# Pooled attention and a feed-forward block on one core: scores of token tile 12 issued before the PSUM pools change, and some 380 other steps placed elsewhere

## The chip, the core and the metric

The kernel runs on one core of one Trainium2 chip. The metric is the device time of one execution in microseconds (us). Five engines work beside each other, each through its own queue in order: TensorE (PE, with its weight loads as PEld), VectorE (DVE), ScalarE (ACT), GpSimd (POOL), and SyncE (SP), which here issues transfers. L790 and the like are lines of the kernel's code.

## What is computed

The inputs are q, k and v with 8 batches, 8 heads, 576 positions and 64 channels, a gain `moe_g_ln` of 512, and two weight matrices, 512 x 2048 and 2048 x 512.

```
k_p, v_p = means of k and of v over groups of 8 positions        # 72 positions
scores   = (q @ k_p.T) / sqrt(64);  scores -= scores.max(-1)
attn     = exp(scores) / (exp(scores).sum(-1) + 1e-9)
x        = (attn @ v_p), heads side by side                      # 4608 tokens x 512
xn       = (x - mean) / sqrt(var + 1e-6) * g_ln
out      = x + relu(xn @ w_ch1) @ w_ch2
```

## The kernel before

**Tiles.** The 4608 tokens are 36 tiles of 128; four tiles make a chunk of 512, so there are nine chunks, c = 0 to 8. The two large products keep float32 accuracy with float16 operands: each operand is split into a high and a low half, and three matmuls stand for one.

**Two lists of steps.** The order of all work is written out by hand, in two strings of tokens, START (the opening, 760 tokens) and STEADY (3404 tokens). A token such as `P.2.0.0.2` names a step and its arguments; each step is a Python generator, and each time that its token stands in the list, `run` (L1410) lets it issue its next piece. So the list gives the order in which every engine's queue receives its instructions, and no engine overtakes its own queue.

**The opening** loads and splits the weights (`R` loads, `C` converts, `M1`, `M2` and `S.m.b` scale and split with ACT L483 and DVE L490), pools the first k and v (`HK`, `HV`), and takes chunks 0 and 1 through with plain products: `F.c.f` is the first product (L1116) and its relu halves (ACT L1125, DVE L1127), `G.c.tt.half` the second (L1319) and its DVE sum into x (L1330).

**The loop over chunks 2 to 8** replaces each large product by seven of half size: `P.c.h.f.m` is one of the seven of the first product (`product`, six matmuls of 256 columns at L1160, then one copy on ACT at L1179 or a sum on DVE at L1174 or L1177 out of PSUM), `EL`, `ER`, `ES`, `EP` build the factors of the second from it (DVE and POOL at L1198, ACT L1196), and `O.c.h.n.u` is one of the seven of the second (`out_seven`, twelve matmuls at L1277, then a DVE sum into x at L1294). Several of the seven share one PSUM tile, so the next product that uses a tile can only start when the copy or sum of the one before has read it.

**Attention.** `A.t` is `stage_a` (L1338) of token tile t: its first piece loads q of tile t + 2, the second issues the 16 score matmuls (L790), the third the row maximum (DVE L800) and the subtraction (DVE L805), and later pieces the exponential, the halves and a transposing transfer. `B.t` is `stage_b`: the matmuls with v, the normalisation (DVE L939 to L961) and what layer norm needs. `TS`, `TW`, `T`, `U`, `WH`, `Z`, `XT` prepare scales and sums of operands.

**PSUM.** The opening uses four pools: `ps_s` for scores and `ps_x`, two banks each, `ps_f` with three and `ps_m` with one. Between the two lists `first.close()` gives them back, and two new pools take the space: `ps_a`, one buffer of two banks (scores and values of the loop), and `ps_g`, six (all products). What the first tile of a new pool writes over must have been read by then.

```
    run(START)
    first.close()
    for name, bufs in (("ps_a", 1), ("ps_g", 6)):
        psum[name] = ctx.enter_context(tc.tile_pool(name=name, bufs=bufs, space=PSUM))
    psum["ps_s"] = psum["ps_x"] = psum["ps_a"]
    psum["ps_f"] = psum["ps_m"] = psum["ps_g"]
    run(STEADY)
```

Of the kernel before, what the change touches and what calls it, by code (L numbers as in the profile page):

```python
# [63 lines left out]
START = """  # L64
LN.2 Q.0 LK.0 LN.2 LK.1 R.1.0 Q.1 A.0 R.1.1 R.1.2 K0 V0 K0 A.0 R.1.3 A.0 A.0 K0 R.1.3 R.1.2 HV.1.0 LK.0 LK.1 LG V0 R.2.0
E.0.0 LG V0 C.1.0 C.1.0 C.1.0 C.1.0 R.2.0 E.0.0 E.0.0 V0 V0 E.0.1 A.1 A.1 V0 A.1 E.1.0 C.1.1 V0 Q.1 C.1.1 E.0.1 C.1.1
C.1.1 E.0.0 V0 V0 C.1.2 C.1.3 E.0.1 C.1.2 E.1.0 E.0.1 E.1.1 HV.1.0 E.1.1 HV.1.0 E.1.1 C.1.3 E.1.1 E.1.0 HV.1.0 E.1.0
R.2.1 HV.1.0 HK.1.0 R.2.1 A.2 A.2 M1.0 A.2 A.2 B.0 A.1 M1.0 M1.0 M1.0 S.1.0 E.2.0 B.0 S.1.0 C.2.0 S.1.1 C.1.2 R.1.1 B.0
E.2.1 Q.0 HV.1.0 S.1.0 A.3 E.2.1 E.2.0 A.3 A.3 C.1.3 S.1.1 HK.1.0 E.2.1 A.3 E.2.0 E.2.1 B.0 B.0 B.0 B.0 S.1.2 E.2.0
R.1.0 B.1 HK.1.0 R.2.2 E.3.0 B.1 R.2.2 E.3.1 E.3.0 E.3.1 E.3.0 E.3.1 B.1 B.1 B.1 B.1 B.1 C.1.3 E.3.1 E.3.0 HV.1.0 C.2.0  # L70
HK.1.0 C.1.2 S.1.2 B.2 B.2 HV.1.1 C.2.2 S.1.3 HV.1.1 C.2.1 B.2 HV.1.0 B.2 B.2 C.2.0 B.2 B.2 S.1.3 HK.1.0 C.2.0 S.1.3 B.3
HK.1.1 HK.1.1 S.1.2 HK.1.1 C.2.1 HK.1.1 HK.1.1 C.2.1 C.2.1 B.3 F.0.0.0 F.0.1.0 F.0.0.0 F.0.1.0 F.0.0.0 R.2.3 D.0 R.2.3
F.0.1.0 A.4 F.0.0.0 F.0.2.0 A.4 F.0.1.0 F.0.3.0 A.4 HV.1.0 HV.1.1 C.2.2 HV.1.1 B.3 C.2.3 F.0.2.0 F.0.3.0 F.0.2.0 A.4
F.0.2.0 A.4 F.0.3.0 F.0.3.0 C.2.3 D.0 F.0.4.0 R.1.4 HV.1.1 A.5 A.5 A.5 C.2.2 C.2.2 HV.1.1 HV.1.1 C.2.3 F.0.4.0 B.3 B.3
B.3 B.3 R.1.4 F.0.5.0 A.5 F.0.6.0 R.1.5 M2.0 M2.0 F.0.5.0 F.0.4.0 F.0.6.0 F.0.4.0 A.5 M2.0 M2.0 R.1.6 S.1.1 A.6 S.2.0
A.6 R.1.7 C.1.4 R.1.7 F.0.5.0 A.4 R.1.5 A.4 HV.1.1 F.0.5.0 F.0.6.0 A.6 S.2.0 F.0.7.0 F.0.0.1 HV.1.1 F.0.0.1 F.0.1.1
HV.1.1 HV.1.1 F.0.1.1 F.0.7.0 HV.1.1 F.0.7.0 HV.1.1 HV.1.1 D.1 D.1 S.2.1 F.0.1.1 C.1.4 F.0.0.1 S.2.1 C.1.7 F.0.2.1 S.2.0
A.7 A.7 R.1.6 C.1.5 F.0.3.1 F.0.3.1 F.0.3.1 C.2.3 F.0.2.1 S.2.2 S.2.2 S.2.2 F.0.2.1 F.0.3.1 HV.1.1 F.0.4.1 F.0.2.1
F.0.5.1 C.1.6 M1.1 F.0.4.1 F.0.5.1 F.0.4.1 F.0.5.1 F.0.5.1 C.1.4 A.6 F.0.4.1 F.0.6.1 B.4 A.5 S.2.3 M1.1 B.4 M1.1 F.0.7.0
A.6 C.1.5 S.2.3 F.0.7.1 F.0.7.1 F.0.7.1 F.0.7.1 G.0.0.0 B.4 F.0.0.1 F.0.1.1 F.0.6.1 S.2.3 C.1.4 A.7 F.0.6.1 C.1.5 A.6  # L80
A.6 S.1.4 G.0.0.0 R.2.4 R.2.4 R.2.5 R.2.5 A.7 C.1.7 B.5 B.4 G.0.1.0 F.0.6.1 A.7 A.7 A.7 B.4 G.0.2.0 C.1.6 C.1.7 C.1.6
S.1.4 R.2.6 R.2.7 S.1.5 B.5 B.5 S.1.5 G.0.1.0 R.2.6 R.2.7 G.0.2.0 G.0.2.0 HK.2.0 G.0.3.0 C.2.4 S.1.6 C.2.5 S.1.6 B.6 B.4
C.2.4 G.0.1.0 B.4 S.1.7 G.0.3.0 S.1.7 F.0.8 HV.2.0 G.0.3.0 B.5 C.2.4 B.5 B.5 F.0.8 B.6 F.0.8 F.0.9 C.2.5 B.5 C.2.6
F.0.10 A.5 C.2.7 C.2.6 F.0.8 F.0.9 F.0.9 F.0.6.0 F.0.11 C.2.5 C.2.7 C.2.5 C.2.6 C.2.7 C.2.7 HK.2.0 F.0.10 C.2.6 F.0.11
B.6 C.2.4 C.1.5 M2.1 S.1.4 F.0.9 HK.2.0 F.0.12 M1.1 HK.2.1 F.0.10 A.8 HK.2.1 HK.2.0 HV.2.0 F.0.10 S.1.7 M2.1 M2.1 S.2.4
S.1.5 F.0.11 HV.2.0 F.0.12 S.2.4 F.0.12 A.8 S.2.5 F.0.12 F.0.13 S.2.4 F.0.11 S.2.5 S.2.5 HK.2.0 HV.2.0 HV.2.0 F.0.13 B.6
F.0.14 HV.2.0 C.1.7 HK.2.1 B.7 HV.2.0 G.0.0.0 S.2.6 F.0.14 HK.2.1 F.0.15 B.6 HK.2.1 F.0.13 F.0.13 S.2.6 S.2.7 S.2.7
F.0.14 F.0.14 F.0.15 S.2.7 HV.2.0 F.0.15 C.1.6 B.7 A.8 B.7 F.0.15 HV.2.0 B.7 A.8 HK.3.0 G.0.0.1 HV.2.1 HK.3.0 HV.2.1 B.7
A.8 HV.2.1 HV.2.1 HV.2.1 B.6 A.8 A.9 G.0.1.1 G.0.2.1 S.1.6 HV.2.1 B.6 B.7 HV.2.1 HV.3.0 G.0.0.1 G.0.1.1 A.9 G.0.2.1 B.7
A.8 A.9 A.9 G.0.3.1 A.9 T.1.0 HV.2.1 A.10 A.10 A.11 A.9 G.0.3.1 T.1.0 G.0.3.1 G.0.3.1 HV.2.1 F.1.0 A.9 B.8 T.1.0 T.1.0  # L90
F.1.0 HK.3.0 A.10 G.0.1.1 G.0.1.1 F.1.1 T.1.0 A.11 B.8 T.1.0 F.1.0 HV.2.1 S.2.6 T.1.0 S.2.1 T.1.0 F.1.2 F.1.0 T.1.0 A.10
T.1.0 HV.2.1 F.1.1 T.1.0 T.1.0 HV.2.1 F.1.1 F.1.2 F.1.2 F.1.3 HV.2.1 F.1.4 F.1.2 F.1.5 HV.2.1 HV.3.0 HV.3.0 T.1.1 HV.2.1
HV.2.1 G.0.2.1 F.1.1 F.1.4 F.1.4 G.0.2.1 HV.3.0 F.1.4 F.1.3 HV.3.0 A.10 A.11 A.10 HV.3.0 F.1.3 T.1.1 A.11 HV.3.0 F.1.3
F.1.6 B.9 F.1.6 T.1.1 F.1.5 HV.3.0 HV.3.0 A.10 T.1.1 A.11 HV.3.1 F.1.5 T.1.1 G.0.0.1 F.1.7 T.1.1 A.11 G.0.0.1 F.1.6
F.1.5 HV.3.1 T.1.1 A.11 HV.3.1 T.1.1 F.1.7 F.1.7 G.1.0.0 G.1.0.0 G.1.0.0 B.9 HV.3.1 G.1.1.0 HV.3.1 F.1.6 T.1.1 HV.3.1
G.1.2.0 HV.3.1 T.1.1 T.1.1 M2.1 HK.3.1 T.1.1 T.0.0 T.0.0 T.0.0 T.0.0 HV.3.1 T.0.0 T.0.0 V.10 G.1.3.0 T.0.0 T.0.0 HK.3.0
HK.3.0 T.0.0 T.0.0 F.1.7 T.0.0 G.1.2.0 HV.3.1 T.0.0 F.1.8 T.0.1 G.1.1.0 F.1.9 T.0.1 F.1.8 T.0.1 G.1.3.0 G.1.3.0 T.0.1
V.10 B.8 B.8 T.0.1 T.0.1 T.0.1 T.0.1 F.1.10 HV.3.1 F.1.8 HV.3.1 F.1.8 HV.3.1 T.0.1 F.1.9 U.0.1 U.0.0 F.1.11 F.1.10
F.1.11 F.1.9 T.0.1 F.1.9 B.8 F.1.10 B.11 B.8 F.1.10 U.0.1 G.1.1.0 F.1.12 B.11 U.0.1 T.0.1 F.1.13 F.1.12 T.0.1 F.1.13
F.1.11 F.1.11 F.1.14 F.1.12 F.1.14 F.1.13 F.1.13 B.9 F.1.15 F.1.15 B.9 U.1.1 B.9 U.1.0 F.1.14 F.1.14 F.1.15 F.1.15 B.9  # L100
B.9 V.10 V.10 HV.3.1 V.10 U.1.0 G.1.0.1 V.10 G.1.1.1 HV.3.1 F.1.12 U.1.0 HK.3.1 HK.3.1 V.10 V.10 G.1.2.1 G.1.0.1 X X
B.11 B.11 B.11 B.11 G.1.1.1 G.1.2.0 G.1.3.1 HV.3.1 HV.3.1 B.11 G.1.0.1 B.11 G.1.0.1 B.11 U.0.0 U.0.0 HK.3.1 HK.3.1 U.1.1
U.1.1 G.1.2.1 G.1.2.1 G.1.2.1 G.1.1.1 G.1.1.1 G.1.3.1 G.1.3.1 G.1.3.1
# [1358 lines left out]
```

## Time and profile before

| what | value |
|---|---|
| median of 3 runs | 791.75 us (791.6 to 792.0) |
| the profiled execution | 792.71 us |
| its span, first to last instruction | 791.0 us |
| PE busy | 772.5 us, 98% |
| PEld, DVE busy | 592.8 us (75%), 628.3 us (79%) |
| ACT, POOL busy | 469.5 us (59%), 492.3 us (62%) |
| TensorE clock granted | full in all 40 slices |

Of the profiled execution 1.7 us lie outside its span. An engine is busy while it executes; its idle time is listed beside the instruction that follows it and what that one waited for. All times within the program count from the span's start. In the timeline, matmuls of 64 rows are listed twice each.

### The profile page before, as it was taken

To read this page: it belongs to the slowest core of one execution; us is meant where nothing else is said; L and a number is where in the kernel's file an instruction comes from. 1 tells how busy PE (TensorE), PEld (TensorE's weight loads), DVE (VectorE), ACT (ScalarE), POOL (GpSimd) and SP (SyncE) were. 2 spreads that over 40 slices of the span, in tenths; PEclk is the share of its full clock that TensorE was granted. 3 is DMA by queue.
4 is the path that set the end of the run, shared out by engine and by line. 5 is a ranking of instruction groups with operands and counts; after the bars stand their busy time and mean duration, and the time that the engine had idled before them with its cause. 6 is when DMAs were issued, how large, how long until landed. Compare 5 with 4: busy or idle time off the path is not lost. (4 is left out here: it accounts for less than half of the span.)

```text
span 791.0 us, 18982 instructions
## 1 busy us (share of the span) xinstructions
PE 772.5 (98%) x7458; PEld 592.8 (75%) x7458; DVE 628.3 (79%) x1296; ACT 469.5 (59%) x880; POOL 492.3 (62%) x597
## 2 busy tenths in 40 slices
...
PEclk9999999999999999999999999999999999999999
...
GB/s 353 302 247 180 252 137 80 170 106 78 43 128 177 151 167 225 186 258 190 204 202 164 241 169 255 151 205 180 228 93 208 176 179 141 175 144 150 81 120 134
DMA packets 181513, 139.01 MB, mean 176 GB/s; under 512 B 143792, under 2 KB 151600, under 8 KB 179248
## 3 DMA queue, kind: packets, MB, share of 16 engines
...
## 5 line engine op out<-in xcount | busy, mean ns | idle before, releaser
L1277 PE MATMUL ps_f<-ring,w 128*128 128x256 f16 x2016 | 231.7, 273 | 1.5 <-DVE x L1294 1.0
L1277 PEld LDWEIGHTS <-w 128*128 128x128 f16 x2016 | 196.2, 98 | 25.8 <-issue 1.8
L1160 PE MATMUL ps_f<-zts,w 128*128 128x256 f16 x1680 | 208.1, 273 | 1.3 <-DVE x L1330 0.8
L1160 PEld LDWEIGHTS <-w 128*128 128x128 f16 x1680 | 162.7, 98 | 22.6 <-issue 2.1
L1319 PE MATMUL ps_f<-w,ring 128*128 128x512 f16 x576 | 126.6, 379 | 0.1
L1319 PEld LDWEIGHTS <-ring 128*128 128x128 f16 x576 | 56.0, 98 | 66.2 <-DVE ring L1127 0.9
L1179 ACT COPY raw<-ps_f 128x256 f32<-128x256 f32 x160 | 56.2, 372 | 81.7 <-PE ps_f L1160 69.3
L1160 PE MATMUL ps_f<-zts,tsp 128*128 128x256 f16 x672 | 92.1, 273 | 0.5 <-DVE raw L1174 0.3
L1116 PE MATMUL ps_f<-zts,w 128*128 128x512 f16 (+1 forms) x480 | 86.5, 336 | 2.9 <-DVE ring L1127 1.6
L1196 ACT CAST w<-w 128x512 f16<-128x512 f32 x96 | 59.0, 619 | 42.3 <-POOL w L1219 24.2
L1116 PEld LDWEIGHTS <-w 128*128 128x128 f16 x480 | 45.8, 98 | 38.8 <-issue 2.7
L1198 POOL TENSOR_TENSOR w<-w 128x512 f16<-128x512 f32 x48 | 57.4, 1197 | 25.5 <-ACT w L1196 22.9
L1160 PEld LDWEIGHTS <-tsp 128*128 128x128 f16 x672 | 64.5, 98 | 8.8 <-issue 0.7
L1215 POOL TENSOR_TENSOR w<-raw 128x256 f32<-128x256 f32 x32 | 25.9, 809 | 64.9 <-ACT raw L1207 42.9
L1294 DVE SCALAR_TENSOR_TENSOR x<-ps_f,y,x 128x256 f32<-128x256 f32 (+1 forms) x84 | 42.6, 518 | 28.5 <-PE ps_f L1277 27.5
L826 POOL TENSOR_TENSOR phl<-e,phl 128x512 f16<-128x512 f32 x32 | 41.1, 1285 | 37.5 <-ACT phl L816 28.9
L1085 POOL TENSOR_TENSOR hl<-raw,hl 128x640 f16<-128x640 f32 x28 | 42.4, 1517 | 17.0 <-ACT hl L1083 16.8
L1294 DVE SCALAR_TENSOR_TENSOR x<-ps_f,cy,x 128x256 f32<-128x256 f32 (+1 forms) x84 | 42.1, 516 | 12.1 <-PE ps_f L1277 11.3
L1198 DVE TENSOR_TENSOR w<-w 128x512 f16<-128x512 f32 x48 | 38.5, 803 | 8.9 <-ACT w L1196 8.9
L1198 DVE TENSOR_TENSOR w<-raw,w 128x512 f16<-128x512 f32 (+1 forms) x64 | 41.6, 654 | 3.3 <-ACT w L1196 3.1
L1179 ACT COPY phl<-ps_f 128x256 f32<-128x256 f32 x64 | 23.1, 372 | 31.9 <-PE ps_f L1160 29.2
L1174 DVE TENSOR_TENSOR raw<-ps_f,raw 128x256 f32<-128x256 f32 x80 | 32.9, 415 | 11.0 <-PE ps_f L1160 7.4
...
## 6 DMA issues: line engine op xcount, KB each, us to landing
...
```

Source lines behind the costliest of these rows:

```text
L826: nc.gpsimd.tensor_tensor(out=ph[:, 0, :, KA:P], in0=e[:, :, 0:KA], in1=ph[:, 0, :, 0:KA], op=ALU.subtract)
L1085: nc.gpsimd.tensor_tensor(out=zhl[:, 1, :], in0=src, in1=zhl[:, 0, :], op=ALU.subtract)
L1116: nc.tensor.matmul(ps, lhsT=w[:, part, fs], rhs=zT[:, kz, cols], start=(n == 0), stop=(n == 3 * NKT - 1),)
L1160: nc.tensor.matmul(ps, lhsT=w[:, part, f * P : (f + 1) * P], rhs=z, start=m in (1, 2, 4, 5) and n == 0, stop=m in (2, 3, 4, 7) and n == 3 ...
L1174: nc.vector.tensor_tensor(out=o, in0=ps, in1=o, op=ALU.add)
L1179: nc.scalar.copy(out=o, in_=ps)
L1196: nc.scalar.copy(out=hi, in_=src)
L1198: engine.tensor_tensor(out=lo, in0=src, in1=hi, op=ALU.subtract)
L1215: nc.gpsimd.tensor_tensor(out=s_tmp[:, 0], in0=r01, in1=r11, op=ALU.add)
L1277: nc.tensor.matmul(ps, lhsT=wt[2][:, left, part, f * HC + u * P : f * HC + (u + 1) * P], rhs=b[:, f // FPB, wp, f % FPB], start=n < 4 and ...
L1294: nc.vector.scalar_tensor_tensor(out=x, in0=ps, scalar=scale, in1=x, op0=ALU.mult, op1=ALU.add)
L1319: nc.tensor.matmul(ps, lhsT=h[:, part, i, cols], rhs=w[:, wp, j], start=(n == 0), stop=(n == 3 * NFT // 2 - 1),)
```

## The change

Three of the seven `A.12` tokens go from the start of STEADY to the end of START: the load of q for tile 14, the 16 score matmuls of tile 12, and the maximum and the subtraction. Since `A.12` is then begun in one list and ended in the other, `run` takes the generators already begun and hands back those that are to be kept open. The matmuls of `A.12` write a buffer of the opening's `ps_s` instead of one of `ps_a`.

```diff
-    def run(tokens):
-        begun = {}
+    def run(tokens, begun, keep=()):
         with tc.manual_schedule():
             for token in tokens.split():
...
-            for steps in begun.values():
-                all_of(steps)
-
-    run(START)
+            for token, steps in begun.items():
+                if token not in keep:
+                    all_of(steps)
+        return {token: begun[token] for token in keep}
+
+    begun = run(START, {}, ("A.12",))
     first.close()
...
-    run(STEADY)
+    run(STEADY, begun)
```

The rest of the diff is the two lists. Their tokens are the same in kind and number; some 270 of START and 1150 of STEADY stand out of the common sequence, mostly by a few places. Two lines of START as an example:

```diff
-B.11 B.11 B.11 B.11 G.1.1.1 G.1.2.0 G.1.3.1 HV.3.1 HV.3.1 B.11 G.1.0.1 B.11 G.1.0.1 B.11 U.0.0 U.0.0 HK.3.1 HK.3.1 U.1.1
-U.1.1 G.1.2.1 G.1.2.1 G.1.2.1 G.1.1.1 G.1.1.1 G.1.3.1 G.1.3.1 G.1.3.1
+G.1.2.1 B.11 B.11 B.11 B.11 G.1.1.1 G.1.2.0 A.12 HV.3.1 A.12 G.1.3.1 HV.3.1 B.11 G.1.0.1 B.11 G.1.0.1 B.11 U.0.0 U.0.0
+HK.3.1 HK.3.1 U.1.1 U.1.1 G.1.2.1 G.1.2.1 G.1.2.1 G.1.1.1 G.1.1.1 G.1.3.1 G.1.3.1 G.1.3.1 A.12
```

No instruction is added or removed on any engine. Three places of the new order follow; tile numbers differ between the two builds.

**PE at the passage from START to STEADY**, before: the score matmuls of `A.12` (L790) stand between two products on the same PSUM tile, `P.2.0.1.1` (weights `w1`) and `P.2.0.1.6` (weights `tsp1`).

```order
L1160 LDWEIGHTS w1_90
L1160 MATMUL ps_f_2687<-zts_94,w1_90 128x256
L790 MATMUL ps_a_2703<-kblk0_113,q_1808 64x72 x16
L1160 LDWEIGHTS tsp1_93
L1160 MATMUL ps_f_2687<-zts_94,tsp1_93 128x256
```

In the change they stand on PE between the last two outputs of the opening, `G.1.1.1` ahead and `G.1.3.1` behind:

```order
L1319 LDWEIGHTS ring_95
L1319 MATMUL ps_f_2561<-w2_91,ring_95 128x512
L790 MATMUL ps_a_2605<-kblk0_113,q_1728 64x72 x16
L1319 LDWEIGHTS ring_95
L1319 MATMUL ps_f_2622<-w2_91,ring_95 128x512
```

The 16 matmuls moved 60 matmuls ahead, past the 24 of `G.1.3.1` and the 36 of the first six products of the loop; `P.2.0.1.6` now follows `P.2.0.1.1` directly. On DVE the two instructions of `A.12` (L800, L805) moved from behind the sum of `P.2.0.1.2` (L1174) to right behind the sum of `G.1.3.1` (L1330).

**DVE in chunk 5**, before: the sum of `O.5.0.4.1` is the last row here, into x_5549, which in the change is x_5556.

```order
L666 TENSOR_REDUCE vp_6265<-vr_7122 72x64
L1294 SCALAR_TENSOR_TENSOR x_5768<-ps_f_7161,cy_6649,x_5768 128x256
L675 TENSOR_REDUCE mv_7196<-vp_6265 72x1
L438 TENSOR_SCALAR rowmax_7198<-mv_7196 72x1
L439 TENSOR_SCALAR rowmax_7198<-rowmax_7198 72x1
L981 TENSOR_SCALAR ln_6779<-ln_6779 128x1
L1198 TENSOR_TENSOR w2_91<-w2_91 128x2x256
L1294 SCALAR_TENSOR_TENSOR x_5768<-ps_f_6943,cy_6649,x_5768 128x512
L1294 SCALAR_TENSOR_TENSOR x_5549<-ps_f_6966,cy_6649,x_5549 128x256
```

In the change, from the same L666 on:

```order
L666 TENSOR_REDUCE vp_6265<-vr_7169 72x64
L1294 SCALAR_TENSOR_TENSOR x_5556<-ps_f_6966,cy_6662,x_5556 128x256
L981 TENSOR_SCALAR ln_6780<-ln_6780 128x1
L1294 SCALAR_TENSOR_TENSOR x_6122<-ps_f_7081,cy_6662,x_6122 128x256
L675 TENSOR_REDUCE mv_7208<-vp_6265 72x1
L438 TENSOR_SCALAR rowmax_7210<-mv_7208 72x1
L439 TENSOR_SCALAR rowmax_7210<-rowmax_7210 72x1
L1294 SCALAR_TENSOR_TENSOR x_5804<-ps_f_7154,cy_6662,x_5804 128x256
```

The sum of `O.5.0.4.1` moved ahead of the pair factor (`EP.5.1.0.0`, the L1198 of the first fence, which in the change comes after the second) and of the 512-column sum of `O.5.0.6.0`.

**DVE in chunk 6**, before: sums of first-product tiles are followed by the low halves of `ER.6.1.1`, `EL.6.1.2` and `EL.6.1.3` (L1198), and then by the normalisation of token tile 31 (`B.31`, L939 to L961).

```order
L1174 TENSOR_TENSOR raw_1800<-ps_f_8656,raw_1800 128x256
L1198 TENSOR_TENSOR w2_91<-phl1_116,w2_91 128x256
L1198 TENSOR_TENSOR w2_91<-raw_1800,w2_91 128x2x256 x2
L1177 TENSOR_TENSOR raw_1800<-ps_f_8470,raw_1800 128x2x256
L1177 TENSOR_TENSOR raw_1800<-ps_f_8576,raw_1800 128x2x256
L939 COPY cvm_8609<-cv_6056 64x3
L939 COPY cvm_8609<-cv_7337 64x3
L940 TENSOR_SCALAR sm_8610<-ps_a_8613,cvm_8609 128x8
```

In the change:

```order
L940 TENSOR_SCALAR sm_8588<-ps_a_8591,cvm_8587 128x8
L948 RECIPROCAL rs_8589<-sm_8588 128x8
L950 TENSOR_TENSOR x_8590<-ps_a_8591,rs_8589 128x512
L960 BN_STATS st_8664<-x_8590 128x6
L961 BN_AGGR ln_7996<-st_8664 128x2
L1174 TENSOR_TENSOR raw_1820<-ps_f_8636,raw_1820 128x256
L1174 TENSOR_TENSOR raw_1820<-ps_f_8465,raw_1820 128x256
L1174 TENSOR_TENSOR raw_1820<-ps_f_8557,raw_1820 128x256
L1174 TENSOR_TENSOR raw_1820<-ps_f_8651,raw_1820 128x256
L1198 TENSOR_TENSOR w2_91<-phl1_116,w2_91 128x256
L1198 TENSOR_TENSOR w2_91<-raw_1820,w2_91 128x2x256 x2
```

All seven instructions of `B.31` moved ahead of four PSUM sums and of the factors of the second product.

## Rows read from the trace of the kernel before

**Rows 1.** The page: busy time by engine, granted clock in 40 slices.

```profile
PE 772.5 (98%) x7458; PEld 592.8 (75%) x7458; DVE 628.3 (79%) x1296; ACT 469.5 (59%) x880; POOL 492.3 (62%) x597
PEclk9999999999999999999999999999999999999999
```

**Rows 2.** Waits of PE over the span: line, releaser, total us, times, longest.

```profile
PE ps_m L723 <- DMA w<-in_kvn_dram: 6.8, 1, 6.8
PE ps_f L1116 <- DVE ring L1127: 1.6, 3, 1.2
PE ps_m L881 <- DVE x L950: 1.0, 1, 1.0
...
PE ps_f L1116 <- DVE w L490: 0.7, 1, 0.7
...
PE ps_f L1160 <- ACT raw L1179: 0.3, 1, 0.3
...
PE ps_a L790 <- DVE e L805: 0.2, 1, 0.2
```

**Rows 3.** Busy time by stretch: length, then PE, PEld, DVE, ACT, POOL.

```profile
80.00:100.00 20.00, 20.00 (x121) 9.65 (x120) 19.16 (x38) 15.00 (x18) 8.57 (x8) 1.00 0.92 265
240.00:260.00 20.00, 19.87 (x257) 16.49 (x256) 19.39 (x44) 13.21 (x29) 17.27 (x24) 1.00 0.78 170
260.00:300.00 40.00, 39.49 (x332) 24.90 (x331) 37.04 (x83) 20.97 (x43) 23.75 (x34) 1.00 0.72 176
```

**Rows 4.** Waits of DVE between 20 and 103 us.

```profile
DVE ring L1127 <- ACT ring L1125: 0.9, 1, 0.9
DVE e L805 <- POOL phl L829: 0.7, 1, 0.7
DVE allmax L478 <- PE ps_m L470: 0.5, 2, 0.3
```

**Rows 5.** Timeline of the opening (start, duration); last, L490's least/median/most ns.

```profile
39.02 3.25 POOL L867 TENSOR_TENSOR pt<-phl,pt 72x512 f16<-72x512 f32 x2
...
40.73 2.63 DVE L490 SCALAR_TENSOR_TENSOR w<-w,gs 128x1024 f16<-128x1024 f32 x1
...
101.32 1.28 DVE L490 SCALAR_TENSOR_TENSOR w<-w,gs 128x1024 f16<-128x1024 f32 x1
...
L490 DVE SCALAR_TENSOR_TENSOR w<-w,gs x8: 1253/1368/2631, 29.6 to 101.3; 128x1024 f16<-128x1024 f32 x8
```

**Rows 6.** Timeline at the passage from opening to loop, DVE, PE and ACT.

```profile
230.91 0.75 DVE L1330 SCALAR_TENSOR_TENSOR x<-ps_f,cy,x 128x512 f32<-128x512 f32 x1 [4.43 <-PE ps_f L1319]
231.72 2.78 PE L1160 MATMUL ps_f<-zts,w 128*128 128x256 f16 x24 [0.84 <-DVE x L1330]
...
233.67 0.42 DVE L1174 TENSOR_TENSOR raw<-ps_f,raw 128x256 f32<-128x256 f32 x1 [2.01 <-ACT raw L1179]
...
235.74 0.73 PE L790 MATMUL ps_a<-kblk,q 64*64 64x72 f32 x32
235.84 0.93 ACT L1179 COPY raw<-ps_f 128x256 f32<-128x256 f32 x3 [2.20 <-PE ps_f L1160]
...
236.59 0.75 DVE L800 TENSOR_REDUCE mx<-ps_a 128x8 f32<-128x576 f32 x1
```

**Rows 7.** Timeline in chunk 5, DVE and PE.

```profile
522.24 1.13 DVE L1294 SCALAR_TENSOR_TENSOR x<-ps_f,cy,x 128x512 f32<-128x512 f32 x2
...
523.43 1.25 PE L1277 MATMUL ps_f<-ring,w 128*128 128x256 f16 x10 [0.69 <-DVE x L1294]
```

**Rows 8.** Timeline in chunk 6, DVE, and PE beside it.

```profile
614.37 1.82 DVE L1198 TENSOR_TENSOR w<-raw,w 128x512 f16<-128x512 f32 x2
...
617.33 0.34 DVE L939 COPY cvm<-cv 64x3 f32<-64x3 f32 x2
...
619.65 0.18 DVE L961 BATCH_NORM_AGGREGATE ln<-st 128x2 f32<-128x6 f32 x1
...
616.12 5.40 PE L1277 MATMUL ps_f<-ring,w 128*128 128x256 f16 x48
```

More of the change, by code (lines that the diff above doesn't have):

```diff
@@ L100 @@
[L100 to L103 removed]
+LN.2 Q.0 LK.0 LN.2 LK.1 K0 R.1.0 Q.1 R.1.1 A.0 R.1.1 R.1.2 R.1.3 R.1.3 K0 K0 V0 A.0 A.0 A.0 HV.1.0 LK.1 LG V0 R.2.0 V0
@@ L104 @@
+G.1.0.1 B.9 B.9 V.10 F.1.14 HV.3.1 V.10 U.1.0 G.1.1.1 HV.3.1 V.10 F.1.12 U.1.0 HK.3.1 HK.3.1 V.10 V.10 G.1.0.1 X X
+G.1.2.1 B.11 B.11 B.11 B.11 G.1.1.1 G.1.2.0 A.12 HV.3.1 A.12 G.1.3.1 HV.3.1 B.11 G.1.0.1 B.11 G.1.0.1 B.11 U.0.0 U.0.0
+HK.3.1 HK.3.1 U.1.1 U.1.1 G.1.2.1 G.1.2.1 G.1.2.1 G.1.1.1 G.1.1.1 G.1.3.1 G.1.3.1 G.1.3.1 A.12
 """
@@ new lines @@
+ER.6.0.3 B.28 P.6.1.0.7 P.6.1.1.5 A.30 A.30 P.6.1.0.7 P.6.1.1.1 O.6.0.0.0 EP.6.0.1.1 P.6.1.0.7 P.6.1.1.5 P.6.1.1.5
+P.6.1.0.3 EP.6.0.1.1 ER.6.0.2 B.28 O.6.0.0.1 EL.6.1.0 ER.6.0.3 LW.6.0.4 EP.6.0.2.0 A.31 EP.6.0.2.0 ES.6.0.2 ES.6.0.2
+EP.6.0.2.1 HK.7.1 HK.7.1 B.28 ER.6.0.3 LW.6.0.4 A.31 P.6.1.1.3 EP.6.0.2.1 O.6.0.0.1 O.6.0.1.1 EP.6.0.2.1 O.6.0.0.0
+O.6.0.1.0 O.6.0.2.1 A.31 O.6.0.2.0 LW.6.0.6 LW.6.0.6 ES.6.0.3 EP.6.0.3.0 A.31 P.6.1.1.1 P.6.1.1.1 HV.7.1 HV.7.1
+O.6.0.2.1 O.6.0.2.1 EP.6.0.3.0 B.30 P.6.1.1.2 EP.6.0.3.0 LW.6.0.5 O.6.0.4.1 O.6.0.2.0 P.6.1.1.6 O.6.0.2.0 P.6.1.1.2
```

591 lines of the change are left out of this document (293 added, 298 removed).

## The prediction

> **What bounds the kernel now.** I read the page first, then the list of what PE waited for, then busy time by stretch, then the timeline where a wait or a moved step stands. The page shows PE busy for 98% of the span at a full clock [rows 1]: 772.5 of 791.0 us. The change adds and removes no instruction, so PE has the same work before and after, and only the idle rest can change. That rest is 18.5 us, of which 6.8 us are one wait for the first transfer [rows 2] that the change doesn't touch. Beside that, PE's list names waits of 0.2 to 1.2 us each [rows 2], and they are what can be won.
>
> They lie in two kinds of stretch. In the opening, from 20 to 103 us, VectorE is the engine without slack: 19.16 busy of 20 us from 80 to 100 us [rows 3], and in all 83 us it waited for other engines only some 2.1 us [rows 4]. PE's waits there are VectorE's work coming late: a relu half (L1127), the normalisation (L950), a weight half (L490) [rows 2]. From 127 us on PE is nearly full, and each wait is a single late sum or copy out of PSUM, one at the passage to the loop and a few inside it.
>
> What a measurement of this kernel can tell from no change is about 0.2%, or 1.6 us.
>
> **The change part by part.** The sum is made against the profiled execution, 792.71 us (span 791.0 and 1.7 around it). That is 0.96 us above the median of the runs, 791.75; I carry each gain or loss over to the median.
>
> *The opening, 20 to 103 us.* Some 270 tokens stand elsewhere. On VectorE, pooling and conversion pieces went behind the normalisation of tile 2, so PE's 1.0 us wait for L950 [rows 2] should go. The 1.2 us wait for the relu half (L1127, the longest of its three) should shrink as well. But the moved VectorE work stands ahead of the next relu halves and the last weight half, whose L490 ends at 102.60 us [rows 5] and lets PE go on, after a 0.7 us wait [rows 2]. The same VectorE work comes before that end in both orders, so the time moves to the next wait. A real gain has to come from VectorE's own waits. If all go, it is 0.9 + 0.7 + 0.5 = 2.1 us [rows 4]; that is the lower end. The upper end is one L490 more of the long kind: 2.63 us at 40.73, beside the POOL instructions that run from 39.02, against 1.28 at 101.32 [rows 5], so 1.35 us more. Neither end is nearer. I take a value near the middle, **-0.5 us**.
>
> *The passage to the loop.* The first product of the loop waits 0.84 us for the last L1330 of the opening [rows 6], since it writes over PSUM which that reads. The score matmuls of `A.12` could fill this hole if they stood between the two. They do not: in the new order they stand ahead of `G.1.3.1`, whose L1330 is the releaser, so everything up to it moves back by their own length (0.73 us), and the 0.84 us stay. What they covered is uncovered: before, they ran from 235.74 while ScalarE copied `P.2.0.1.1` out of PSUM (the first of three copies that begin at 235.84 and take 0.93 us together) [rows 6], and `P.2.0.1.6` needs that copy. Now `P.2.0.1.6` follows at once. With no cover PE waits from about 235.7 until a third of those 0.93 us has passed and been signalled, about 236.25: **+0.55 us**. The ends are +0.3 (one copy alone) and +0.7 (all of the old cover).
>
> The other half of the move is on VectorE. Its maximum and subtraction took 0.75 us each at 236.59 and after. They now run right behind the L1330 that ends at 231.66, in a hole of 2.01 us [rows 6], and cost nothing there: the next instruction, at 233.67, waits for ScalarE. That takes 1.5 us out of a dense stretch: VectorE is busy for 19.39 of 20 us and 37.04 of 40 afterwards, while PE loses 0.13 + 0.51 = 0.64 us [rows 3]. I take all of it, **-0.64 us** (ends -0.64 and 0). Were the hole not there, the 1.5 us would delay the first sum of the loop. The passage as a whole: about **-0.1 us**. The load of q for tile 14 is issued on SyncE's queue, which runs far ahead here; nothing.
>
> *Chunk 5, 523 us.* PE waits 0.69 us for the sum of `O.5.0.4.1`, the last of the two that run from 522.24 [rows 7]. In the new order this sum stands ahead of a factor (L1198) and a 512-column sum, right behind an L666, and its product is long done. It ends several microseconds before PE wants the bank: **-0.7 us** (ends -0.69 and 0, if the wait passes to the next sum).
>
> *Chunk 6, 617 us.* The seven instructions of `B.31` run from 617.33 to 619.83, 2.5 us [rows 8]. Before, they came behind the factors of the second product, whose last L1198 ended at 616.2. In the new order they stand ahead of four sums and of these factors. The factors end 2.5 us later, less what VectorE idled between: about 618.0. PE began the 48 matmuls of that product at 616.12, each 5.40 / 48 = 0.11 us, and its twelfth, at 616.12 + 11 x 0.11 = 617.3, is the first to use the low half of the last factor [rows 8]. So a new wait of 0.7 us. Against it, the 0.2 us for which scores waited for a subtraction (L805) [rows 2] goes, as does a little behind it. Net **+0.4 us** (ends -0.2, if the factors keep up, and +0.7).
>
> *The rest.* The 0.3 us wait for a copy in chunk 8 (ACT L1179) [rows 2] goes, and the same copy of a neighbouring tile becomes late in its place by as much. Two further products, at 113 and 333 us, lose their slack and wait 0.2 to 0.3 us each, by the nearest row, that same 0.3 [rows 2]. Net **+0.3 us** (ends -0.3 and +0.7). At the end two outputs change places and the last product stays the last: **-0.1 us** (ends -0.3, 0).
>
> **Sum:** -0.5 - 0.1 - 0.7 + 0.4 + 0.3 - 0.1 = -0.7 us. Against the profiled execution this is 792.0; against the median, 791.75 - 0.7 = **791.05 us**, no difference that can be told.
>
> **The rivals.**
>
> *1. VectorE's waits in the opening go.* If the new order feeds VectorE without a hole between 20 and 103 us, the opening gives 2.1 us instead of 0.5, and with the other terms at -0.2 the time is 791.75 - 2.3 = 789.45. For it: one of PE's largest waits goes by the new order, and 2.1 us is all in three rows [rows 4]. Against it: PE was full from 80 to 100 us [rows 3], so what VectorE gains before that must also carry through the chain to the last weight half.
>
> *2. The loop's waits go and no new ones come.* Then the passage's dense stretch gives -0.64, chunk 5 -0.69, the scores -0.2 and the copy in chunk 8 -0.3; with -0.4 of the opening and the tail the sum is -2.2 and the time 789.55. For it: each has its row. Against it: the two new waits that I expect (the uncovered copy, the factors behind `B.31`) follow from the order by arithmetic.
>
> *3. Slower: long L490 in the opening.* A VectorE instruction of this line took 2.63 us beside a POOL stretch, where the median of the eight in the opening is 1.37 and the last took 1.28 [rows 5], with VectorE the bound. The new order pairs them with other POOL work. From two more of the long kind on, 2 x 1.35 = 2.7, and with the other terms (-0.2) the time is 791.75 + 2.5 = 794.25. Fewer of the long kind would be part of rival 1's gain. For it: nothing in the lists of steps keeps these two engines apart. Against it: with a median of 1.37, at least four of the eight were short before [rows 5].
>
> The Trainium skill states a rule on this (SBUF — State Buffer, the section on SBUF's two separate sides): VectorE and GpSimd share one pair of ports under an exclusive lock, so that an instruction with two SBUF inputs and a GpSimd instruction don't share bandwidth, one blocks until the other is done. By that rule the long L490 sat out a whole GpSimd instruction, and the opening could come out either way with the neighbours that the new order gives each; the trace agrees with it in the one long case, 2.63 against 1.28 us [rows 5].
>
> *4. The change does not do what it says*, if the score matmuls were meant to fill the hole at the passage. It is in my forecast: the 0.84 us [rows 6] stay.
>
> **How the numbers follow.** My forecast has a chance of 0.40 and covers no change, with its own range of 790.2 to 793.3. Rival 1 has 0.26 and rival 2 0.14: both are faster by over 0.2% (below 790.17). Rival 3 and what is like it, a chain of new waits in the loop, has 0.20 (above 793.33). So faster 0.40, same 0.40, slower 0.20. The range reaches down past the two faster rivals, to 788.9, and up to the edge of rival 3, 793.5: it leaves about 0.08 below and 0.12 above. The bounds of the single terms add up to more (-3.9 and +3.5 us), but they won't fall on one side together.
>
> **What would show it.** In the profile of the changed kernel: PE's wait for L1330 at the first product of the loop is still about 0.8 us; a wait for an L1179 copy of some 0.5 us stands three to five microseconds behind it; L800 and L805 stand right behind that L1330 on VectorE; the 0.7 us wait at 523 us is gone; a wait for L1198 appears near 617 us; the three VectorE waits of the opening add up to about 1.6 us; and the first matmul behind the weight half near 102.6 us starts within half a microsecond of where it did. Wrong would be: that matmul over 1.5 us earlier (rival 1) or over 1 us later with two or more L490 above 2 us (rival 3), or no new wait at the passage and near 617 us (rival 2).

## The result, and the profile after

The changed kernel took **795.99 us** (median of 7 runs, 794.07 to 799.58), the kernel before in the same session 791.86 (7 runs, 789.71 to 792.47). The ratio is 1.006, with a 95% interval of 1.0038 to 1.0081. It is taken from the means, and makes 4.7 us (3.0 to 6.4); the medians, which are used from here on, differ by 4.1 us. Two of the seven runs (799.58 and 797.33 us) had a granted clock of 0.997 and 0.998, and without them the median is 795.97. The forecast was 791.05 with a range up to 793.5, so the time lies above all of it.

The profiled execution took 794.46 us, which is near the fastest of the seven; 1.5 us of the median's loss are therefore not in this trace. The page of the changed kernel, busy time by engine:

```profile
span 792.7 us, 18979 instructions
PE 771.9 (97%) x7458; PEld 592.4 (75%) x7458; DVE 629.9 (79%) x1296; ACT 468.7 (59%) x880; POOL 493.4 (62%) x597
PEclk9999999999999999999999999999999999999999
```

The work and the clock are those of before [rows 1], so what was added is idle time of PE. What PE waited for in the changed kernel (line, releaser, total us, times, longest), to be read against [rows 2]:

```profile
PE ps_f L1160 <- DMA zts<-hl: 3.1, 2, 1.6
PE ps_f L1116 <- DVE ring L1127: 2.3, 3, 1.4
PE ps_f L1160 <- DVE x L1330: 0.8, 1, 0.8
PE ps_f L470 <- DVE rowmax L439: 0.8, 1, 0.8
...
PE ps_m L470 <- DVE rowmax L439: 0.7, 1, 0.7
...
PE ps_f L1160 <- ACT raw L1179: 0.5, 1, 0.5
```

The first row is new in kind. `zts` is the transposed sum of two token tiles that the loop's products read (step `XT`), and a transposing transfer on SyncE's queue brings it. PE waits for it twice, 1.45 us at 475 us in chunk 4 and 1.65 us at 712 us in chunk 8. Neither place is in the prediction. The two rows of L470 are new too. That of `ps_m` is at 26 us, where PE waits for a small chain of VectorE instructions that takes the maximum of the first weights, by which they are scaled; before, PE did not wait there. That of `ps_f` is at 270.6 us, in the loop, and belongs to the passage below.

**Chunk 4.** SyncE's queue and PE in the kernel before:

```profile
467.20 0.40 SPq L659 DMA_DIRECT2D vr<-in_v_dram  x1
469.57 2.19 SPq L1076 DMA_TRANSPOSE zts<-hl  x1
471.81 0.59 SPq L645 DMA_DIRECT2D kr<-in_kT_dram  x1
474.29 0.82 PE L1160 MATMUL ps_f<-zts,w 128*128 128x256 f16 x6
```

and in the changed kernel:

```profile
467.04 0.43 SPq L645 DMA_DIRECT2D kr<-in_kT_dram  x1
469.41 1.34 SPq L1076 DMA_TRANSPOSE zts<-hl  x1
470.85 0.49 SPq L659 DMA_DIRECT2D vr<-in_v_dram  x1
475.74 0.83 PE L1160 MATMUL ps_f<-zts,w 128*128 128x256 f16 x6 [1.45 <-DMA zts<-hl]
```

The load of k (288 KB) and that of v (144 KB) have changed places around the transposing transfer. It is issued 0.16 us earlier than before, but its data came 6.3 us after the issue, where it had come after 3.7 us. PE wanted it at 474.29 in both builds. So up to here the change had cost PE nothing, and from here on it is 1.45 us late.

**Chunk 8.** Before:

```profile
703.59 0.32 SPq L1266 DMA_DIRECT2D ring<-w2s  x1
706.97 1.50 SPq L1076 DMA_TRANSPOSE zts<-hl  x1
713.72 0.82 PE L1160 MATMUL ps_f<-zts,w 128*128 128x256 f16 x6
```

Changed kernel:

```profile
705.12 0.32 SPq L1266 DMA_DIRECT2D ring<-w2s  x1
705.53 2.33 SPq L1076 DMA_TRANSPOSE zts<-hl  x1
711.98 0.83 PE L1160 MATMUL ps_f<-zts,w 128*128 128x256 f16 x6 [1.65 <-DMA zts<-hl]
```

Here the transposing transfer is issued earlier against the loads, 0.41 us behind one of 512 KB instead of 3.4 us behind it. But it takes 6.4 us to land where it took 3.0 before (709.99), so that little is won. And the product that reads it, `P.8.0.0.4`, stands ahead of pieces of the second product that it stood behind. PE came to it at 711.98 - 1.65 = 710.33, 3.4 us earlier than before, in spite of what it had lost by then.

**The first 28 us.** VectorE's chain for the first weights and POOL beside it, before:

```profile
24.52 0.17 DVE L562 TENSOR_SCALAR wm<-wm 128x4 f32<-128x4 f32 x1
...
25.13 0.16 DVE L571 TENSOR_TENSOR t<-wm,g_sb 128x4 f32<-128x4 f32 x1
26.49 2.28 POOL L867 TENSOR_TENSOR pt<-phl,pt 72x512 f16<-72x512 f32 x2 [1.01 <-ACT pt L865]
```

and in the changed kernel, with PE:

```profile
24.20 0.17 DVE L562 TENSOR_SCALAR wm<-wm 128x4 f32<-128x4 f32 x1
...
24.62 1.08 DVE L571 TENSOR_TENSOR t<-wm,g_sb 128x4 f32<-128x4 f32 x1
24.52 2.27 POOL L867 TENSOR_TENSOR pt<-phl,pt 72x512 f16<-72x512 f32 x2
26.32 0.23 PE L470 MATMUL ps_m<-ident,rowmax 128*128 128x128 bf16 x1 [0.66 <-DVE rowmax L439]
```

POOL's L867, a piece of step `E`, moved ahead by 2 us, and now runs beside the chain. An instruction on 128x4 elements that took 0.16 us takes 1.08; it ends at 25.70, 0.03 us after the first of POOL's pair.

**The terms that came as forecast.** At the passage, after:

```profile
231.75 0.75 DVE L800 TENSOR_REDUCE mx<-ps_a 128x8 f32<-128x576 f32 x1
231.89 2.78 PE L1160 MATMUL ps_f<-zts,w 128*128 128x256 f16 x24 [0.84 <-DVE x L1330]
236.44 0.38 PE L1160 MATMUL ps_f<-zts,tsp 128*128 128x256 f16 x2 [0.46 <-ACT raw L1179]
```

The 0.84 us wait is still there [rows 6], the uncovered copy costs 0.46, and the maximum stands right behind the L1330. Busy time by stretch behind it (length, then PE, PEld, DVE, ACT, POOL):

```profile
240.00:260.00 20.00, 20.00 (x259) 16.61 (x258) 19.39 (x40) 14.33 (x31) 17.13 (x24) 1.00 0.85 181
260.00:300.00 40.00, 39.23 (x333) 25.01 (x332) 36.67 (x88) 19.82 (x41) 25.24 (x35) 1.00 0.76 183
```

PE gained 0.13 us in the first stretch and lost 0.26 in the second [rows 3]; of the 0.64 us that I had counted on, nothing is left. The waits that I had counted are gone, a wait of 0.30 us for a sum (L1174) at 266 us among them. But all 0.77 us that PE idles in the second stretch are one new wait, that of L470 for L439 at 270.6 us: a short chain on VectorE (L675, L438, L439), the maximum of a piece of pooled v, now reaches PE late.

### The profile page after: what moved, and what is told of

The parts are those of the page before. It is cut to its first block, busy times and chain, and to the rows that moved or that the text cites. A ratio compares the mean times of both kernels' runs of the same rounds, so it can differ in the third digit from the quotient of the medians.

```text
span 792.7 us, 18979 instructions
## 1 busy us (share of the span) xinstructions
PE 771.9 (97%) x7458; PEld 592.4 (75%) x7458; DVE 629.9 (79%) x1296; ACT 468.7 (59%) x880; POOL 493.4 (62%) x597
## 4 chain that ended last, share of the span: by engine, by line
PE 77%; DVE 12%; ACT 4%; DMA 3%; POOL 3%; issue 1%; DVEq 0%; POOLq 0%
PE ps_f L1160 28%; PE ps_f L1277 23%; PE ps_f L1319 12%; PE ps_f L1116 8%; PE ps_a L790 2%; DMA zts<-hl 2%; DVE w L543 2%; DVE w L490 1%; PE ps_a L932 1%; PE ps_a L933 1%; ACT w L1196 1%; PE ps_m L723 1%; DMA ring<-w2s 1%; DMA w<-in_kvn_dram 1%; DVE wm L527 1%
## 5 line engine op out<-in xcount | busy, mean ns | idle before, releaser
L1198 POOL TENSOR_TENSOR w<-w 128x512 f16<-128x512 f32 x48 | 58.0, 1208 | 26.2 <-ACT w L1196 25.3
L1198 DVE TENSOR_TENSOR w<-raw,w 128x512 f16<-128x512 f32 (+1 forms) x64 | 43.6, 686 | 3.3 <-ACT w L1196 2.9
L1198 DVE TENSOR_TENSOR w<-w 128x512 f16<-128x512 f32 x48 | 38.1, 793 | 6.2 <-ACT w L1196 6.2
L1174 DVE TENSOR_TENSOR raw<-ps_f,raw 128x256 f32<-128x256 f32 x80 | 32.2, 414 | 12.2 <-PE ps_f L1160 9.3
```

What stands on the lines that cost most here:

```text
L1174: nc.vector.tensor_tensor(out=o, in0=ps, in1=o, op=ALU.add)
L1198: engine.tensor_tensor(out=lo, in0=src, in1=hi, op=ALU.subtract)
```

## The experiments

Each comparison is with the kernel before in the same session. "Behind before" is the difference of the medians. In the kernels e6, e8, e9 and e12 line numbers are one lower than in the other builds.

**e1: the order of chunk 4's loads put back.** On the changed kernel:

```diff
-LW.4.1.4 XT.22.1
+XT.22.1 LW.4.1.4
...
-HK.6.1 O.4.1.4.0 A.24 XT.23.0 HV.7.0
+O.4.1.4.0 A.24 HV.7.0 XT.23.0 HK.6.1
```

> The changed kernel with SyncE's order around the end of chunk 4 as before: the v load of HV.7.0 ahead of the transposing transfer XT.23.0 and the k load of HK.6.1 behind it, and the ring load LW.4.1.4 behind XT.22.1; all other steps as changed. Theory (two transposing transfers land late behind loads that were moved ahead of them): PE's wait of 1.45 us for zts near 475 us goes, the one near 712 us stays, and the median falls by 1.4 us or more against the changed kernel, to about 794 us. Rival (PE's engines: the uncovered copy at the passage and VectorE work in the loop cost the time): the wait may go, but the median stays within 1 us of the changed kernel's 796.

Measured: 794.44 us (8 runs), ratio 1.0028 (1.0018 to 1.0037), 2.7 us behind before instead of 4.1. The wait at 475 us is gone, that of chunk 8 stays with 1.58 us. So this order held some 1.4 us of the loss.

**e2: chunk 7's loads of weights in the other order**, on the changed kernel; the theory was that a late ring load pushes chunk 8's transfer back.

```diff
-LW.7.1.4 LW.7.1.4 LW.7.1.5
+LW.7.1.5 LW.7.1.4 LW.7.1.4
```

> The changed kernel with one pair of tokens as before: the ring load LW.7.1.5 ahead of LW.7.1.4, so that the load whose buffer comes free first is not held by the other. Theory: PE's wait of 1.65 us for zts near 712 us goes, the one near 475 us stays, and the median falls by 1.5 us or more against the changed kernel, to about 794 us. Rival: the median stays within 1 us of the changed kernel's 796.

Measured: 796.19 us (5 runs), ratio 1.0053 (1.0041 to 1.0065). Both waits for `zts` stay, 2.53 and 1.38 us. The theory fell.

**e3: both edits.**

> The changed kernel with both places of SyncE's order as before. Theory: both waits for zts go and the time is that of before less what the trace of the changed kernel gained elsewhere (792.71 + 1.75 - 3.1 gives 1.4 us less than before): a median of 790 to 791.5 us, and a spread of the runs as small as that of before. Rival: 795 to 796 us, as the changed kernel.

Measured: 793.42 us (9 runs), ratio 1.0023 (1.0011 to 1.0034), 1.7 us behind before: a miss, since neither the 790 to 791.5 us of the theory nor the rival's time came. With both loads in their old order, chunk 8 of e3 shows:

```profile
703.35 0.32 SPq L1266 DMA_DIRECT2D ring<-w2s  x1
...
710.16 0.83 PE L1160 MATMUL ps_f<-zts,w 128*128 128x256 f16 x6 [1.60 <-DMA zts<-hl]
```

The wait of chunk 8 does not hang on the order of these loads. With chunk 4's loss undone the two builds stand close enough in time here to be laid side by side. The data arrive as they did before: issued at 703.76 instead of 706.97, they are there at 710.11 instead of 709.99. But PE comes to the product at 710.16 - 1.60 = 708.56, 5.2 us earlier than before. So the cause of this wait is to be looked for in PE's order.

**e4: the kernel before with the changed kernel's three orders of loads.**

```diff
-XT.22.1 LW.4.1.4
+LW.4.1.4 XT.22.1
...
-HV.7.0 XT.23.0 HK.6.1
+HK.6.1 XT.23.0 HV.7.0
...
-LW.7.1.5 LW.7.1.4
+LW.7.1.4 LW.7.1.5
```

> The kernel before with nothing but the three swaps of SyncE's tokens of the changed kernel (HK.6.1 and HV.7.0 around XT.23.0, LW.4.1.4 ahead of XT.22.1, LW.7.1.4 ahead of LW.7.1.5). Theory: waits for zts near 475 and 712 us appear, 3 us together, and the median is 794.5 to 796.5 us. Rival: 791.5 to 792.5 us, as before.

Measured: 793.45 us (11 runs), ratio 1.0024 (1.0016 to 1.0033). PE waits for `zts` once, 1.22 us at 476.00 us, and not in chunk 8. So chunk 4's order makes its wait in either kernel, whatever else differs: shown from both sides. Which of its two swaps does it was not taken apart: in the changed kernel the ring load ahead landed 1.46 us later as well (472.01 us against 470.55).

**e5: e1, and `P.8.0.0.4` begun where the kernel before begins it.**

```diff
-EP.7.1.3.1 P.8.0.0.4 O.7.1.4.1
+EP.7.1.3.1 O.7.1.4.1
...
-O.7.1.6.0 O.7.1.6.1
+O.7.1.6.0 P.8.0.0.4 O.7.1.6.1
```

> The changed kernel with SyncE's order around chunk 4 as before (as in the first experiment) and with the matmuls of P.8.0.0.4 put behind those of O.7.1.6.0, about where they stood before; the ring loads LW.7.1.4 and LW.7.1.5 stay in the changed order. Second theory (the wait near 712 us is not made by the ring loads but by P.8.0.0.4, which reads the tile of XT.35.0 and was moved four products ahead of where it stood, in front of that transfer's landing): no wait for zts is left and the median is 791 to 792.3 us. Rival (the transfer would be late wherever it is read, or VectorE and ScalarE waits cost the rest): a wait of 1 us or more stays near 712 us, and the median is 793 us or more.

Measured: 792.67 us (11 runs), ratio 1.0007 (0.9996 to 1.0017). No wait for `zts` is left. Against e1, from which it differs by one token, it stands 2.1 us better (2.7 behind before, now 0.6), uncertain by about 1.1. So one step of PE, taken 5 us earlier, cost about 2 us; the wait itself was 1.6. The forecast time (791 to 792.3) was missed all the same, and so was the rival's.

**e6: the move of `A.12` alone**, on the kernel before.

```diff
-G.1.1.1 G.1.2.0 G.1.3.1
+G.1.1.1 G.1.2.0 A.12 A.12 G.1.3.1
...
-A.12 A.12 P.2.0.1.6
+P.2.0.1.6
```

The third `A.12` goes to the end of START likewise.

> The kernel before with the move of the three A.12 tokens alone. My forecast for this part was +0.55 us for the uncovered copy and -0.64 us for VectorE's dense stretch behind it: a wait for ScalarE's L1179 of 0.46 us near 236 us as in the changed kernel, the wait of 0.30 us for L1174 near 266 us gone, and a median of 791.5 to 792.1 us. Rival (the move itself costs what the changed kernel lost): 793 us or more.

Measured: 792.65 us (11 runs), ratio 1.0005 (0.9996 to 1.0014): no difference that can be told, though just above the forecast's 791.5 to 792.1. The wait for the uncovered copy appears, and in the dense stretch behind it a 0.3 us wait for a sum stays as before. The move that names the change did neither good nor harm.

**e7: `P.8.0.0.4` early, in the kernel before.**

```diff
-O.7.1.1.0 O.7.1.6.1
+O.7.1.1.0 P.8.0.0.4 O.7.1.6.1
```

> The kernel before with one token moved: the matmuls of P.8.0.0.4 ahead of those of O.7.1.6.1, near the place that the change gives them. Second theory: a wait for zts of about 1 us or more appears near 711 us, and the median is 792.5 to 793.5 us. Rival (the ring loads): no such wait, 791.5 to 792.3 us.

Measured: 792.33 us (11 runs), ratio 1.0005 (0.9996 to 1.0014), and no wait for `zts`. PE, then SyncE's queue, in e7:

```profile
710.40 0.83 PE L1160 MATMUL ps_f<-zts,w 128*128 128x256 f16 x6
...
707.39 1.53 SPq L1076 DMA_TRANSPOSE zts<-hl  x1
```

A miss, by my choice of the place: it is later than the change's, and PE came to the product when the data had just landed, 3.0 us after the issue. So the step may move 3.7 us ahead at no cost (713.72 before, and e7 runs 0.4 us later here), and loses from about there on. That it loses at the change's own place, some 1.5 us further ahead, only e5 and e1 show.

**e8: the changed START with STEADY of before**, so all of the change up to 231 us and nothing behind it.

> The changed START list (with A.12 moved) in front of the STEADY list of before. Theory (the opening neither gains nor loses, and the loss lies in the loop): the first product behind the weight half near 102.5 us starts within 0.5 us of before, and the median is 791 to 792.5 us. Rival (the opening loses in the runs that no profile shows): 794 us or more.

Measured: 794.24 us (6 runs, 791.80 to 794.95), ratio 1.0031 (1.0019 to 1.0043). The opening loses 2.2 us, though in the profiled execution, at 791.80 the fastest of the six, there is next to nothing of it. What that trace has is the stretched L571 at 24.65 us, in e8 numbered L570.

**e9: e8 with START's first 84 tokens as before**, up to the fourth `M1.0`, the chain on the first weights; the rest of START keeps the change's order. A piece of it:

```diff
-V0 E.1.1 V0 C.1.3 V0 E.0.1 E.1.1 E.0.1 HV.1.0 R.1.2 E.1.0
+V0 V0 C.1.2 C.1.3 E.0.1 C.1.2 E.1.0 E.0.1 E.1.1 HV.1.0 E.1.1 HV.1.0
...
```

> The eighth experiment (changed START, STEADY of before) with the first 84 tokens of START, up to the scale chain of the first weight (M1.0, some 28 us), in the order of before and the rest of START as changed. Theory (the changed first tokens put POOL's L867 beside the chain of small VectorE instructions L562 to L576, which then take 0.7 to 1.1 us each instead of 0.2, and all that follows is late by 1 to 2.5 us, by the execution): L571 takes under 0.4 us in the profile, and the median is about 2 us below that of the eighth experiment, 791.5 to 792.8 us. Rival (the order of the opening behind 28 us costs it): 793.5 us or more.

Measured: 791.06 us (11 runs), ratio 0.9999 (0.9990 to 1.0007). The loss is gone, 2.7 us with these 84 tokens. POOL's instruction waits for ScalarE again and lies behind the chain. From the timeline of e9:

```profile
25.21 0.16 DVE L570 TENSOR_TENSOR t<-wm,g_sb 128x4 f32<-128x4 f32 x1
26.19 2.27 POOL L866 TENSOR_TENSOR pt<-phl,pt 72x512 f16<-72x512 f32 x2 [1.25 <-ACT pt L864]
```

**e12: e8 once more, for a second profile of the same program.**

> The eighth experiment once more, for a second profile, since its first profile was its fastest execution (791.8 us) and the others took 793.8 to 795.0 us. Theory: where this execution takes over 793.5 us, the additional time stands in front of the weight half near 102 us, with small VectorE instructions (L562 to L571) of 0.7 us or more beside POOL's L867. Rival (the loop of this build varies): the weight half starts near 102.4 us as in the first profile, and waits for transfers appear behind it.

Measured: 793.74 us, a span of 792.0 where e8's was 790.1. PE at the end of the chain, first in e8:

```profile
26.35 0.23 PE L469 MATMUL ps_m<-ident,rowmax 128*128 128x128 bf16 x1 [0.66 <-DVE rowmax L438]
```

then VectorE's L489 (in the other builds L490), the chain, POOL and PE in e12:

```profile
22.86 1.23 DVE L489 SCALAR_TENSOR_TENSOR vb<-vp,sv,vh 72x512 f16<-72x512 f32 x1
...
25.25 0.69 DVE L561 TENSOR_SCALAR wm<-wm 128x4 f32<-128x4 f32 x1
25.97 1.08 DVE L562 TENSOR_SCALAR wm<-wm 128x4 int32<-128x4 int32 x1
27.09 0.65 DVE L570 TENSOR_TENSOR t<-wm,g_sb 128x4 f32<-128x4 f32 x1
24.75 2.28 POOL L866 TENSOR_TENSOR pt<-phl,pt 72x512 f16<-72x512 f32 x2
26.99 0.73 POOL L668 TENSOR_TENSOR vr<-vr 72x256 f32<-72x256 f32 x1
28.37 0.23 PE L469 MATMUL ps_m<-ident,rowmax 128*128 128x128 bf16 x1 [1.66 <-DVE rowmax L438]
```

and the start of the chain in e8:

```profile
24.24 0.17 DVE L561 TENSOR_SCALAR wm<-wm 128x4 f32<-128x4 f32 x1
```

Three instructions of the chain instead of one are stretched, and it ends 2.02 us later. The chain's own part of that is 1.0 us (0.69 + 1.08 + 0.65 against 0.17 + 0.18 + 1.08); the rest is its start, 25.25 against 24.24 us. Of this, 0.5 us is the L489 at 22.86, which took 0.74 in e8 and 1.23 here beside POOL's L668 (in e8 it was the L668 that came out longer, 0.96 instead of 0.74 us), and 0.5 us was lost before 14 us. So about 1.5 us is VectorE beside POOL. Each stretched instruction of the chain ends 0.02 to 0.04 us after an instruction of POOL does. The last weight half of the opening, at 104.43 instead of 102.44 us, carries the 2 us whole to the loop, and from there on the two executions run alike. Of the seven profiles of builds with the changed first 84 tokens, PE waits here for 0.6 to 0.7 us in four (the change, e1, e3, e8) and for 1.7 to 1.8 in three (e2, e5, e12); in the seven with the old ones L571 takes 0.16 us. So the loss of the first 28 us depends on how the two engines happen to meet, which would also explain why the profiled execution of the changed kernel, with 0.66 us here, stands below its median.

**e10: all three places put back**, that is e5 with the first 84 tokens of START as in e9; the rest of the change stays.

> The changed kernel with all three places put back: first 84 tokens of START, SyncE's order around chunk 4, P.8.0.0.4 in chunk 8. Theory: no wait for zts, no long L571, and with the waits that the change removed (0.7 us at 523 us and some 0.8 us more) a median of 790.3 to 791.8 us. Rival (something else in the changed lists costs time): 792.5 us or more.

Measured: **790.48 us** (11 runs, 789.41 to 791.25), ratio 0.9987 (0.9978 to 0.9995). It is faster than both kernels, than the one before by 1.05 us (0.4 to 1.7). PE's waits:

```profile
PE ps_f L1116 <- DVE ring L1127: 1.9, 2, 1.4
...
PE ps_f L470 <- DVE rowmax L439: 0.8, 1, 0.8
...
PE ps_f L1277 <- DMA ring<-w2s: 0.6, 1, 0.6
```

No `zts`, and no 0.7 us at 26 us; the 0.8 us at 270 us stays. The last weight half ends its wait at 101.94 us, 0.72 earlier than before.

**e11: START of before with e5's loop** (the three `A.12` back at its beginning), to tell what the changed loop is worth by itself.

> START of before, and the changed STEADY with the two loop places put back and the three A.12 tokens at the beginning of STEADY again. Theory: as the kernel before, less the waits at 523, 629, 705 and 730 us (0.69 + 0.19 + 0.33 + 0.27), plus the new wait of 0.78 us at 271 us: 790.8 to 791.7 us, 0 to 1 us below before. Rival (the removed waits come back elsewhere): no difference, 791.7 to 792.3 us.

Measured: 793.66 us (7 runs), ratio 1.003 (1.0018 to 1.0041). A miss: I expected it near before. Its profile (795.34 us, the slowest of the seven) has a new wait of 2.0 us, and 1.6 us in two waits for loads of `ring` (0.4 at 554.6 us and 1.25 at 629.7), which were not followed.

```profile
PE ps_f L1160 <- ACT raw L1179: 2.0, 1, 2.0
```

It stands at 248.61 us, soon after the place where `A.12` went back in. VectorE has the maximum and the subtraction of `A.12` (0.75 and 0.76 us) at 237.34 again, and comes later to what follows. Two small instructions (L1047, L1048) then lie beside POOL's L1252 and take 0.49 and 1.08 us instead of 0.15 and 0.16, and a group of four behind them nearly doubles, first in e10, then in e11:

```profile
239.19 1.48 DVE L1239 TENSOR_TENSOR kr<-w 128x256 f32<-128x256 f16 x4
241.71 2.80 DVE L1239 TENSOR_TENSOR kr<-w 128x256 f32<-128x256 f16 x4
```

The sum behind it (L1174) begins at 244.43 us instead of 240.59, on ScalarE an L1186 waits 2.25 us for it, and the copy that PE needs stands behind that L1186. So the changed order of the loop seems to lean on `A.12` being done early, which would make the move worth something after all with that loop, though nothing with the old one (e6). This is read from one trace of each build, and e10 and e11 differ in the rest of START as well.

**The account.** Each step undoes one place, and each median is set against before in its own session:

| kernel | us behind before | what the step gave |
|---|---|---|
| the change | 4.13 | |
| e1, chunk 4's order put back | 2.68 | 1.45 |
| e5, also `P.8.0.0.4` | 0.62 | 2.06 |
| e10, also the first 84 tokens | -1.05 | 1.67 |

The three places make 5.2 us of loss, and what is left of the change is a gain of 1.05 us. The single steps are uncertain, the first by nearly 2 us and the others by about 1.1, as the intervals say. Chunk 4's order gave 1.45 us here, 2.8 between e2 and e3, and 1.7 on the kernel before (e4); the first 84 tokens gave 2.7 us between e8 and e9 and 1.7 between e5 and e10.

## Why the prediction was wrong

**Opening, -0.5 us.** The named waits went as forecast in part: that for L950 is gone [rows 2], the weight half starts 0.29 us earlier (102.37 against 102.66). But the relu halves cost 2.3 us instead of 1.6, and VectorE's own three waits, 2.1 us before and forecast at about 1.6, came to 3.3 (2.1, 0.7 and 0.5). With the first 84 tokens put back the weight half starts 0.72 us earlier (e10), so -0.5 was a fair size for what I looked at. The step that failed is its stretch, "from 20 to 103 us" with L490 as the only line that can stretch. The chain at 24 to 28 us lay inside it, and I did not set POOL's moved instructions beside it: 1.7 us by e10, 2.7 by e9.

**Rival 3** had the mechanism, VectorE stretched beside POOL with the order of the lists as its only guard, and a time (794.25) that e8 met at 794.24. But its instruction was wrong: the longest L490 of the opening was 1.85 us after the change and 2.63 before [rows 5]. The size agrees by chance. What stretched was a chain of instructions of 0.2 us, which a list ordered by busy time does not show, and which has PE waiting at its end (in e12 also an L490, but the short one of 72x512, for 0.5 us).

The Trainium skill (SBUF — State Buffer, SBUF: two separate sides) says that a VectorE instruction with two inputs in SBUF, or in a two-port mode, and a GpSimd instruction exclude each other for a whole instruction. The trace agrees for L571, which reads `wm` and `g_sb`: 1.08 us beside L867, one of whose pair takes 2.27 / 2 = 1.14, and 0.16 without it. In e12 L561 and L562, with one tensor as input each, stretch as well; whether they run in a two-port mode no row shows.

**Passage, -0.1 us.** The wait that stays (0.84) and the uncovered copy (0.46 for a forecast of 0.55) are right. The relief of VectorE (-0.64) failed: the stretch gave 0.13 and took 0.26. The waits that it counted did go in the change, but with the move alone (e6) the wait of 0.3 us for a sum stays, and in the changed loop 0.78 us for L439 came in their place, also in e10. The error is to have taken all that PE idled there as due to VectorE's load, and to have looked for no new wait behind the passage.

**"The load of q for tile 14 is issued on SyncE's queue, which runs far ahead here; nothing."** True of that load, and the step that failed for chunk 4: I followed no other load on this queue. Two loads and a transposing transfer change order at 467 us, and PE had no slack for it: 1.45 us. The order alone would have shown the swap; the trace shows that PE took the transfer's data 1 us after it had come (473.30 against 474.29), which was the bound that I should have worked out.

The Trainium skill (DMA: Bandwidth & Descriptors, Two DMAs through the same engine are not ordered) says that within a queue of one DMA engine descriptors start in order. The trace agrees in so far as the transfer behind a 288 KB load came 6.3 us after its issue, and 3.7 behind one of 144 KB.

**Chunk 5, -0.7 us.** The wait is gone, but that the new order removed it is not shown. The second product in the change, and in e6, which has chunk 5's old order:

```profile
518.96 5.40 PE L1277 MATMUL ps_f<-ring,w 128*128 128x256 f16 x48
519.42 5.40 PE L1276 MATMUL ps_f<-ring,w 128*128 128x256 f16 x48
```

In none of the six builds that keep the old order here (e4, e6, e7, e8, e9, e12) does the 0.69 us wait stand. In the profile of before, VectorE's factor ahead of the sum had itself waited for ScalarE:

```profile
521.09 1.23 DVE L1198 TENSOR_TENSOR w<-w 128x512 f16<-128x512 f32 x1 [1.33 <-ACT w L1196]
```

So the term was read from one execution, and that it came as forecast is luck: no run shows that the medians owe anything to it.

**Chunk 6, +0.4 us.** Wrong, harmlessly: the last L1198 ended at 617.94, about as forecast, but PE began the product 0.9 us later, at 617.04, and its twelfth matmul at 617.04 + 11 x 0.11 = 618.25. PE did so because of what it had lost before, in chunk 4 above all: the same 5754 matmuls stand ahead in both builds. But e10, which has not lost that, does not wait either: its product starts at 615.36, and the factor ends at 616.26, 0.3 us before it is needed and hardly later than before (616.19). So the step that failed is the 2.5 us: `B.31` ran in time in which VectorE had idled, 1.8 us of it a wait for ScalarE at 611 us.

**"The rest", +0.3 us.** The copy in chunk 8 did not become late, and the products at 113 and 333 us did not wait; the end gave 0.06 us for a forecast of 0.1. What I overlooked in the same chunk is `P.8.0.0.4`, 5 us earlier on PE and reading a tile that is still on its way: 2.06 us by e5.

**The range** let one place go wrong at a time; "they won't fall on one side together" was said of the terms that I had, and three that I had not fell on one side. The 4.1 us are rival 3's mechanism on other instructions and its "chain of new waits in the loop" at once. In rival 2 the opening and the tail stand at -0.4, where the terms give -0.5 - 0.1; its time would be 789.35.
